# Attention with a third buffer for two copies, a second one for the inverted sums, and divisions planned later

## The chip, the cores and the metric

The kernel runs on one core of one Trainium2 chip. The number that counts is the device time of one execution, in microseconds (us). A core has a matrix engine (TensorE, "PE" in the profile, with its weight loads as "PEld"), a vector engine (VectorE, "DVE"), a scalar engine (ScalarE, "ACT"), a general one (GpSimd, "POOL") and a queue that issues transfers (SyncE, "SP"). Each works through its own list of instructions in order, and they wait for one another by semaphores.

## The reference

The input x has 2048 tokens of 576 numbers. After a layer norm two branches are computed and joined:

```
xn  = layernorm(x)
s   = attention(xn): 32 heads of 18, each token sees itself and the 255 before it
      p = softmax(q k^T / sqrt(18) in the window);  o = p v;  s = o @ wo
z   = gelu(xn @ w_in);  z1, z2 = halves of 2304 columns;  z2 = layernorm(z2)
g   = silu((z1 * (w_sp @ z2 + b_sp)) @ w_out)
out = x + s * g
```

The change lies in the attention. What matters of it: scores, their maximum, the exponential, the product P.V, and the division of P.V by the sum of the exponentials.

## The kernel before, in words

The program has stages. First q, k, v and z2 are made, until some 430 us. Then comes the attention stage, from 434 to about 884 us, in which the z1 half of `w_in` is computed as well. Then o is multiplied by `wo` (from 892 to 954 us), then come the spatial product with `w_sp` and the output product.

In the attention stage the work is cut into 16 units: 8 groups of 4 heads, times two halves of 1024 tokens (`UNITS`, `NU` = 16; the first 8 units are the first half). For each unit

- the maxima of the scores are computed ahead, 32 times a matmul (`max_item`, line 600) and a reduction on VectorE (line 604); `max_split` (613, 614) and `max_end` (623, 626) turn them into two rows that SP moves beside q (`move`, line 630);
- `scores` makes score tiles again (line 724), ScalarE takes their exponential into `pt` (line 728), GpSimd masks the diagonal and the far edge of the window (lines 736 and 739);
- `pv` multiplies with v into a PSUM tile `ops` (line 752). There is one such tile; after four blocks of tokens ScalarE copies it into one half of the unit's tile `ou` (line 767), so that a unit has two such copies. A column of ones in v gives the sums of the exponentials in the same tile;
- after the second copy `finish` plans the rest: SP takes the sums out of `ou` into `den` (814), VectorE inverts them (`invert`, 787), SP stores them (789) and reads them back spread over the partitions into `rp` (`sums`, 794), GpSimd multiplies `ou` by `rp` in four parts (`divide`, 798), and SP stores the four heads' rows to `o_d` (`store`, 803).

TensorE is filled up in between with z1: two rows of matmuls (`z1_rows`, line 671), each on half of the partitions, into one PSUM bank each (`ma` and `mb`). After 27 matmuls ScalarE copies the bank into a tile `z1o` (line 676), there are 72 such copies, and SP stores it (line 573 in the profile, where `tick` runs what is due).

The order of all this is written out when the program is built, by a planner in the same file: it keeps a clock of its own, `spend` adds TensorE's time to it, `use` keeps a planned time at which each other engine is free, and `after(ns, job)` puts a job on a list `waiting`, from which `tick` takes what is due. At each step the planner takes P.V work whose masks it believes done (`pv_now`, with the due times in `todo`), else a score or a maximum, else a matmul of z1. What comes out is a fixed order of instructions on each engine. On the chip an engine that has to wait holds all that is behind it in that order.

A tile of a pool has a number of buffers (`bufs`). When a tile is asked for again after that many times, its first writer waits until all work on the earlier tile in that buffer is done. So ScalarE's copy into `ou` of a unit waits for the stores of the unit two before it, and its copy into `z1o` for the store of the copy two before it. The work on the earlier tile must also come earlier in the program; that is what the `while parts.get(u - 2): part(u - 2)` lines are for, which put out what the planner had not yet put out.

`parts[u]` are the unit's eight late jobs, four divisions and four stores, and the times in `DIVIDE_AT` are those after the end of the unit at which they fall due, one after the other.

Of the kernel before, what the change touches and what calls it, by code (L numbers as in the profile page):

```python
# [46 lines left out]
LOAD_STEP = 700  # L47
INVERT_AT = 6500
FETCH_AT = 8500
DIVIDE_AT = (20000, 21200, 22400, 23600, 26500, 27000, 27500, 28000)  # L50
WARM = 54
SPB = 3
PTB = 5
# [6 lines left out]
def f32(ap):  # L60
    return ap.bitcast(F32)
# [3 lines left out]
def kernel(  # L65
# [170 lines left out]
    with ExitStack() as early:  # L236
# [283 lines left out]
        with ExitStack() as ph:  # L520
# [37 lines left out]
            def after(ns, fn):  # L558
                waiting.append((clock + ns, fn))
# [7 lines left out]
                return busy[engine] + drain  # L567

            def tick():
                for w in list(waiting):  # L570
                    if w[0] <= clock:
                        waiting.remove(w)
                        w[1]()
# [85 lines left out]
            def z1_rows(r):  # L659

                for f in range(FH // P):
                    z1_at[r] = f
                    if f not in z1w:
                        z1w[f] = load_z1(f)
                    wh, wl, jobs = z1w[f]
                    while jobs:
                        jobs.pop(0)[0]()
                    for b in range(2):
                        ps = fillp.tile([P, 512], F32, name=("ma", "mb")[r])
                        for n, (w, x_) in enumerate(moving_x(wh, wl, slice(b * 512, (b + 1) * 512), r)):  # L670
                            pe.matmul(ps, w, x_, start=n == 0, stop=n == STEPS - 1)  # L671
                            spend(r, MM + 3)
                            z1_done[r] += 1
                            if n == STEPS - 1:
                                zo = zw.tile([P, 512], F32, name="z1o", bufs=2)
                                act.activation(zo, ps, AF.Copy)  # L676
                                bank_free[r] = use("act", 480, 120) + 100
                                after(bank_free[r] - clock + KEEP_NS,
                                      partial(sp.dma_start, z1_tokens[f * P:(f + 1) * P, b, :, r],
                                              zo.rearrange("p (a q) -> p a q", a=2)))  # L680
                            if f + 1 < FH // P and min(z1_at) == f:
                                if b == 0 and n == 0 and f + 1 not in z1w:
                                    z1w[f + 1] = load_z1(f + 1)
                                if b == 1 and n % 4 == 2 and f + 1 in z1w and z1w[f + 1][2]:
                                    job, engine, ns = z1w[f + 1][2].pop(0)
                                    job()
                                    use(engine, ns)
                            yield
# [53 lines left out]
            def pv(u, kb, qa, qz):  # L742
                g, half = UNITS[u]
                pt = pts[u, kb]
                k0 = 0 if half == 0 else 6
                c = qa // 4
                first = max(4 * c - 2, 0)
                if kb == first:
                    o_ps[c] = ops.tile([P, 512], F32, name="ops")
                hi = min(4 * c + 3, qz)  # L750
                for j in range(4):
                    pe.matmul(o_ps[c][32 * j:32 * j + 32, (qa - 4 * c) * P:(hi - 4 * c + 1) * P],  # L752
                              vgs[u][:, kb - k0, j * VW:j * VW + 32], pt[:, j, (qa - kb) * P:(hi - kb + 1) * P],
                              start=kb == first, stop=kb == 4 * c + 3, skip_group_check=True)
                spend_both((hi - qa + 1) * 218)
                if hi == qz:
                    pts.pop((u, kb))
                else:
                    later.append([0.0, u, kb, hi + 1, qz])
                if kb == 4 * c + 3:  # L760
                    if c % 2 == 0:
                        while parts.get(u - 2):
                            part(u - 2)
                        ous[u] = (ap_.tile([P, HS], F32, name="ou", bufs=2) if u < NU - 1 else
                                  tail()[:, 0:HS])
                    ou = ous[u]
                    act.activation(ou[:, c % 2 * 512:c % 2 * 512 + 512], o_ps.pop(c), AF.Copy)
                    free_at = use("act", 500, 120)
                    for t in later:
                        t[0] = free_at  # L770
                    if c % 2 == 1:
                        finish(u, ou)
# [3 lines left out]
            def part(u):  # L776
                if parts[u]:
                    parts[u].pop(0)()

            def finish(u, ou):  # L780

                g, half = UNITS[u]
                cs = slice(half * HS, half * HS + HS)
                den = aa.tile([P, HS // 32], F32, name="den")
                rp = ap_.tile([P, HS], F32, name="rp", bufs=1) if u < NU - 1 else f32(slots[4][:, 0:HS])
                def invert():
                    dve.reciprocal(den, den)
                    t = use("dve", 270) - clock + 300
# [16 lines left out]
                if u == NU - 1:  # L805
                    def put_last():
                        dve.reciprocal(den, den)
                        sp.dma_start(r_d[u].rearrange("h (a b) -> (h a) b", b=HS // 32), den)

                    last.extend([lambda: sp.dma_start(den, ou[DH::32, :]), put_last,  # L810
                                 lambda: [sums(i) for i in range(4)], lambda: [divide(a, 2) for a in range(2)],
                                 lambda: [store(i) for i in range(4)]])
                else:
                    after(busy["act"] - clock + 1000, lambda: sp.dma_start(den, ou[DH::32, :]))
                    sooner = 10000 if u == NU - 2 else 0
                    after(max(INVERT_AT - sooner, 4500), invert)
                    parts[u] = [partial(divide, a) for a in range(4)] + [partial(store, i) for i in range(4)]
                    for ns in DIVIDE_AT:
                        after(ns - sooner + (3500 if sooner else 0), partial(part, u))

            def sp_combos(stack):

# [180 lines left out]
            with ExitStack() as heads:  # L1003
# [64 lines left out]
                while score_queue[0] or score_queue[1] or todo or filling:  # L1068
# [37 lines left out]
                        wo_splits.pop(0)()  # L1106
                    if u == NU - 1 and n % 4 == 0 and n // 4 < 5:
                        if n == 0:
                            while parts.get(u - 2):
                                part(u - 2)  # L1110
                            wors = [tail()[:, HS:HS + D],
                                    ap_.tile([P, HS], F32, name="ou", bufs=2)[:, :D]]
                        if n == 8:
                            wors.append(ap_.tile([P, 10, 89], F32, name="vg").rearrange("p a b -> p (a b)")[:, :D])
                        load_wo(n // 4)
# [572 lines left out]
```

## Time and profile before

| what | us |
|---|---|
| runs of the kernel | 1860.76, 1861.42, 1868.03; median 1861.42 |
| the profiled execution, its own time | 1859.38 |
| its span, first to last instruction | 1857.3 |
| TensorE busy in the span | 1823.3 |
| attention stage, 434 to 884 us: TensorE busy of 450.0 | 437.48 |
| mean granted clock of TensorE over the span | 0.994 |

A row of a timeline gives the start, the duration, the engine, the line of the program and the operation, `out<-in` by tile names, and in brackets how long the engine stood idle before it and on what. In a table of waits the columns are who waited for whom, the total in us, how often, and the longest. In a table of windows each engine has its busy time and its count of instructions; the last three columns are TensorE's granted clock, the share of the transfer engines that was busy, and GB/s. An engine name with a q is its queue.

### The profile page before, as it was taken

Reading aid. Unit: us, or ns where it says so; the run is one execution under the profiler, and the core shown is the slowest. Engines: PE = TensorE matmul, PEld = TensorE weight load, DVE = VectorE, ACT = ScalarE, POOL = GpSimd, SP = SyncE. Lnnn points to the kernel's source line nnn. Section 1 sums busy time; section 2 is a strip of 40 time slices with the busy share of each in tenths; the row PEclk is TensorE's granted clock in tenths of the full one; section 3 lists DMA queues with packets and bytes.
Section 4 is the critical chain, followed back from the end, with each engine's and each line's share of the span. In section 5 each row is a group of like instructions: output and inputs, shape, how many; then the busy total and the mean of one; then the engine's idle time right before and its main releaser. Section 6 shows DMA issues by size and latency. Waiting matters only on the chain.

```text
span 1857.3 us, 38172 instructions
## 1 busy us (share of the span) xinstructions
PE 1823.3 (98%) x14363; PEld 1590.3 (86%) x14363; DVE 1138.2 (61%) x2289; ACT 947.8 (51%) x1758; POOL 430.7 (23%) x507
## 2 busy tenths in 40 slices
PE   8999999999999999999999999999999999999998
PEld 8999999997777777776898878888888888899998
DVE  6321333467766677771246788667876567758876
ACT  5433322225666576667467566465554544444443
POOL 3332333334465455556100000111100000000000
PEclk9999999999999999999999999999999999999999
DMA  8885688887566666754776777789777656786554
GB/s 254 206 229 169 232 278 281 290 258 224 154 194 168 187 174 179 189 161 142 239 266 225 236 239 244 258 293 302 252 262 234 185 183 198 250 266 187 160 159 134
DMA packets 266920, 405.75 MB, mean 218 GB/s; under 512 B 52336, under 2 KB 180592, under 8 KB 266608
## 3 DMA queue, kind: packets, MB, share of 16 engines
q1 hardware_dynamic: 266736, 403.32, 70.4%
q8 instruction: 113, 1.85, 0.4%
q14 instruction: 71, 0.58, 0.1%
HBM read 285.35 MB, written 117.09 MB: 217 GB/s over the span
## 4 chain that ended last, share of the span: by engine, by line
PE 82%; DVE 7%; DMA 5%; SPq 2%; ACT 2%; issue 2%; POOL 0%; DVEq 0%; ACTq 0%; POOLq 0%
PE acc L1431 34%; PE mb L206 11%; PE c L1522 7%; PE ma L671 6%; PE mb L671 5%; PE ma L206 5%; PE ops L752 4%; PE tps L724 3%; PE sp L600 3%; PE wops L1157 2%; SPq L363 1%; DMA st_d<-qkhl 1%; DVE junk L604 1%; DVE spl L116 1%; PE ma L380 0%
## 5 line engine op out<-in xcount | busy, mean ns | idle before, releaser
L1431 PE MATMUL acc<-spl,zh 128*128 128x512 f32 x1008 | 392.6, 390 | 1.1 <-DVE spl L116 0.9
L1431 PE MATMUL acc<-sph,zh 128*128 128x512 f32 x1008 | 392.2, 389 | 0.0
L1431 PE MATMUL acc<-sph,zl 128*128 128x512 f32 x1008 | 392.1, 389 | 0.0
L604 DVE CUSTOM_DVE_ANT_0 junk<-sp,band 128x384 bf16<-128x384 f32 (+1 forms) x512 | 276.4, 540 | 114.9 <-PE sp L600 33.6
L728 ACT ACTIVATE pt<-tps 128x384 f32<-128x384 f32 (+2 forms) x576 | 231.2, 441 | 121.6 <-PE tps L724 78.0
L116 DVE TENSOR_TENSOR spl<-spr,sph 128x1024 fp32r<-128x1024 f32 x168 | 210.2, 1251 | 40.0 <-ACT sph L115 39.3
L671 PE MATMUL mb<-b,z1wh 64*128 64x512 f32 x648 | 225.2, 400 | 2.5 <-ACT z1o L676 2.1
L671 PE MATMUL ma<-b,z1wh 64*128 64x512 f32 x648 | 224.8, 399 | 0.6 <-ACT zt L948 0.4
L1431 PEld LDWEIGHTS acc<-spl,zh 128*128 128x128 f32 x1008 | 189.2, 188 | 41.7 <-DVE spl L116 2.8
L1431 PEld LDWEIGHTS acc<-sph,zh 128*128 128x128 f32 x1008 | 189.3, 188 | 39.3
L1431 PEld LDWEIGHTS acc<-sph,zl 128*128 128x128 f32 x1008 | 189.3, 188 | 39.3
L115 ACT ACTIVATE zh<-b 128x384 fp32r<-128x384 f32 x168 | 87.3, 520 | 211.1 <-PE acc L1431 206.7
L115 ACT ACTIVATE sph<-spr 128x1024 fp32r<-128x1024 f32 x168 | 176.0, 1048 | 14.5 <-DMA spr<-in_w_sp_dram 5.3
L724 PE MATMUL tps<-att 56*128 56x384 f32 (+1 forms) x576 | 177.2, 345 | 2.2 <-ACT pt L728 1.2
L116 DVE TENSOR_TENSOR zl<-b,zh 128x384 fp32r<-128x384 f32 x168 | 99.6, 593 | 124.0 <-ACT zh L115 123.9
L600 PE MATMUL sp<-att 54*128 54x384 f32 (+1 forms) x512 | 161.2, 349 | 2.0 <-DVE mx L604 1.8
L1522 PE MATMUL c<-b,o 128*128 128x288 f32 x1056 | 143.3, 295 | 0.5 <-DVE o L116 0.5
L1522 PEld LDWEIGHTS c<-b,o 128*128 128x128 f32 x1056 | 141.0, 188 | 0.8 <-DVE o L116 0.7
L949 DVE BATCH_NORM_STATS2 st<-zt 128x6 f32<-128x384 f32 x96 | 49.3, 548 | 132.1 <-ACT zt L948 132.0
L671 PE MATMUL ma<-b,z1wl 64*128 64x512 f32 x324 | 128.4, 396 | 0.0
L671 PE MATMUL mb<-b,z1wl 64*128 64x512 f32 x324 | 127.8, 394 | 0.0
L724 PEld LDWEIGHTS tps<-att 56*128 56x128 f32 x576 | 99.7, 184 | 30.5 <-issue 9.5
(219 smaller groups left out, 4189.6 us busy)
## 6 DMA issues: line engine op xcount, KB each, us to landing
spr<-sc_d SPq DMA_DIRECT2D x96, 512.0 KB
spr<-in_w_sp_dram SPq DMA_DIRECT2D x72, 512.0 KB
zr<-z_d SPq DMA_DIRECT2D x144, 192.0 KB
z_d<-zt SPq DMA_DIRECT2D x48, 384.0 KB
z_d<-z1o SPq DMA_DIRECT2D x72, 256.0 KB
z1t<-z_d SPq DMA_DIRECT2D x72, 256.0 KB
y_d<-z1t SPq DMA_DIRECT2D x72, 256.0 KB
a<-in_w_sp_dram SPq DMA_DIRECT2D x64, 256.0 KB
```

Source lines behind the costliest of these rows:

```text
L115: act.activation(hi, src, AF.Copy)
L116: dve.tensor_tensor(lo, src, f32(hi), ALU.subtract)
L206: pe.matmul(banks[h][:, :n], *both[h][i], start=i == 0, stop=i == STEPS - 1)
L600: pe.matmul(ps[:, :w], q_of(u, j)[0:54, i * P:(i + 1) * P], k_of(u, j)[0:54, k0:k0 + w], start=True, stop=True)
L604: dve.tensor_tensor_reduce(out=junk[:, :w], in0=ps[:, :w], in1=band[:, m0:m0 + w], scale=1.0, scalar=-3.0e38, op0=ALU.add, op1=ALU.max, ac ...
L671: pe.matmul(ps, w, x_, start=n == 0, stop=n == STEPS - 1)
L724: pe.matmul(ps[:, :m * P], k_of(u, j)[:, (kb - base) * P:(kb - base + 1) * P], q_of(u, j)[:, (a - lo) * P:(a - lo + m) * P], start=True, s ...
L728: act.activation(pt[:, j, d0:d0 + n * P], ps[:, (qa - a) * P:(qa - a + n) * P], AF.Exp, scale=scale)
L752: pe.matmul(o_ps[c][32 * j:32 * j + 32, (qa - 4 * c) * P:(hi - 4 * c + 1) * P], vgs[u][:, kb - k0, j * VW:j * VW + 32], pt[:, j, (qa - kb) ...
L949: dve.bn_stats(st2[:, s, pc, :], zv)
L1431: pe.matmul(acc[j], z[:, ps], w[:, cs], start=s == i == 0 and n in OPENS, stop=s == 7 and i == 2, skip_group_check=True)
L1522: pe.matmul(banks[key][:, :288], y, w, start=begin and k == n == 0, stop=close and k == 8 and n == 2, skip_group_check=True)
```

## The change

- `ou`, the copy of P.V, has three buffers and not two, `z1o`, the copy of z1, has three and not two, and `rp`, the inverted sums spread over the partitions, has two and not one. The lines that put out late jobs before a buffer is taken again go by the unit three back for `ou`, and a new line puts out the divisions of the unit two back before `rp` is taken.
- The four divisions of a unit fall due 24.0 to 27.6 us behind its end and not 20.0 to 23.6, its four stores 33 to 36 us behind and not 26.5 to 28.0. For the unit before the last (`sooner`) the divisions keep their times, 13.5 to 17.1, and the stores come at 22.5 to 25.5 and not at 20.0 to 21.5.
- At the start of the last unit the parts put out are those of unit 12 and not of unit 13; the second tile there for a piece of `wo` is one of the three `ou` buffers.
- `tick` takes what is due in the order of the due times and not in the order in which it was put on the list.

```diff
-DIVIDE_AT = (20000, 21200, 22400, 23600, 26500, 27000, 27500, 28000)
+DIVIDE_AT = (24000, 25200, 26400, 27600, 33000, 34000, 35000, 36000)
...
             def tick():
-                for w in list(waiting):
+                for w in sorted(waiting, key=lambda w: w[0]):
...
-                                zo = zw.tile([P, 512], F32, name="z1o", bufs=2)
+                                zo = zw.tile([P, 512], F32, name="z1o", bufs=3)
...
-                        while parts.get(u - 2):
-                            part(u - 2)
-                        ous[u] = (ap_.tile([P, HS], F32, name="ou", bufs=2) if u < NU - 1 else
+                        while parts.get(u - 3):
+                            part(u - 3)
+                        ous[u] = (ap_.tile([P, HS], F32, name="ou", bufs=3) if u < NU - 1 else
...
+                while len(parts.get(u - 2, ())) > 4:
+                    part(u - 2)
                 den = aa.tile([P, HS // 32], F32, name="den")
-                rp = ap_.tile([P, HS], F32, name="rp", bufs=1) if u < NU - 1 else f32(slots[4][:, 0:HS])
+                rp = ap_.tile([P, HS], F32, name="rp", bufs=2) if u < NU - 1 else f32(slots[4][:, 0:HS])
...
                     for ns in DIVIDE_AT:
-                        after(ns - sooner + (3500 if sooner else 0), partial(part, u))
+                        after(ns - (10500 if sooner else 0), partial(part, u))
...
-                            while parts.get(u - 2):
-                                part(u - 2)
+                            while parts.get(u - 3):
+                                part(u - 3)
                             wors = [tail()[:, HS:HS + D],
-                                    ap_.tile([P, HS], F32, name="ou", bufs=2)[:, :D]]
+                                    ap_.tile([P, HS], F32, name="ou", bufs=3)[:, :D]]
```

## The prediction

> **What bounds the kernel now.** I read the page's busy times first, then windows over the attention stage, where the whole change lies, then TensorE's waits in that stage, and then the timeline around each of them.
>
> ```profile
> PE 1823.3 (98%) x14363; PEld 1590.3 (86%) x14363; DVE 1138.2 (61%) x2289; ACT 947.8 (51%) x1758; POOL 430.7 (23%) x507
> ...
> 434.00:884.00 450.00, 437.48 (x4316) 333.79 (x4316) 287.28 (x1022) 298.08 (x734) 238.56 (x350) 1.00 0.63 174
> ...
> PE sp L623 <- DVE ms L614: 2.9, 5, 0.9
> PE mb L671 <- ACT z1o L676: 2.1, 4, 1.5
> PE ops L752 <- ACT ou L767: 2.0, 2, 1.1
> PE ops L752 <- issue: 1.7, 2, 0.9
> PE tps L724 <- ACT pt L728: 1.2, 3, 0.8
> PE ops L752 <- POOL ou L798: 0.8, 1, 0.8
> PE tps L724 <- DMA att<-mhl: 0.7, 1, 0.7
> ```
>
> TensorE is the bound, and its order is fixed when the program is built. In the attention stage it stood idle for 450.0 - 437.5 = 12.5 us, and no change that leaves TensorE's work as it is can win more there than that and what a lower clock costs. The change adds no instruction and removes none: it moves 120 of them and takes waits for buffers away. So the question is which of the waits above are waits for a buffer. The names on the right don't say it, since ScalarE and GpSimd are themselves held up by something. Two of the waits are.
>
> The first is the longest of the two behind `ACT ou`:
>
> ```profile
> 583.89 0.32 SPq L803 DMA_DIRECT2D o_d<-ou  x1
> ...
> 589.73 0.60 ACT L767 ACTIVATE ou<-ops 128x512 f32<-128x512 f32 x1 [1.29 <-DMA r_d<-den]
> ...
> 590.38 0.86 PE L752 MATMUL ops<-pt,vg 128*32 128x128 f32 x16 [1.11 <-ACT ou L767]
> ```
>
> ScalarE's copy at 589.73 is the first of unit 5, into the buffer that unit 3 used. It waited 1.29 us for a transfer. The profile names the store of the inverted sums, but a copy into `ou` needs nothing of those; what it needs is that the last store out of that buffer has landed, the one issued at 583.89. So that store took 5.8 us to land or a little less, and TensorE lost 1.11 us.
>
> The second is the longest behind `ACT z1o`:
>
> ```profile
> 628.19 0.60 ACT L676 ACTIVATE z1o<-mb 128x512 f32<-128x512 f32 x1 [4.33 <-PE mb L671]
> 628.83 0.60 ACT L676 ACTIVATE z1o<-ma 128x512 f32<-128x512 f32 x1
> ...
> 633.32 7.21 DMA z_d<-z1o
> ...
> 640.63 0.60 ACT L676 ACTIVATE z1o<-mb 128x512 f32<-128x512 f32 x1 [1.60 <-DMA z_d<-z1o]
> ...
> 641.28 0.49 PE L671 MATMUL mb<-b,z1wh 64*128 64x512 f32 x1 [1.54 <-ACT z1o L676]
> ...
> 642.00:643.00 1.00, 1.00 (x8) 0.88 (x7) 0.45 (x3) 1.00 (x3) 0.00 (x1) 0.59 0.59 181
> 643.00:644.00 1.00, 1.00 (x8) 0.85 (x8) 0.54 (x2) 1.00 (x3) 1.00 (x2) 0.50 0.70 194
> 644.00:645.00 1.00, 1.00 (x8) 1.00 (x6) 0.57 (x2) 0.60 (x3) 1.00 (x2) 0.50 0.70 111
> 645.00:646.00 1.00, 1.00 (x10) 0.95 (x7) 0.36 (x1) 0.50 (x2) 0.19 (x1) 0.70 1.33 189
> ```
>
> The copies at 628.19 and 628.83 took both buffers. The store of the first was issued at 633.32, 4.5 us after that copy ended, and took 7.21 us. The third copy had to wait, and TensorE, whose bank it was to empty, stood for 1.54 us. Then the granted clock (third number from the right) was below one in four windows: they lost 0.41 + 0.50 + 0.50 + 0.30 = 1.71 us of full clock. I count both to this wait: 3.25 us.
>
> The rest of the waits are of other kinds. These rows look like GpSimd's and like nobody's:
>
> ```profile
> 666.03 0.43 PE L752 MATMUL ops<-pt,vg 128*32 128x128 f32 x8 [0.76 <-POOL ou L798]
> ...
> 721.22 0.60 ACT L767 ACTIVATE ou<-ops 128x512 f32<-128x512 f32 x1
> ...
> 721.93 0.86 PE L752 MATMUL ops<-pt,vg 128*32 128x128 f32 x16 [0.89 <-issue]
> ```
>
> At 721.93 TensorE began the next unit's P.V 0.11 us after ScalarE had emptied the only `ops` tile (721.22 + 0.60 = 721.82). The wait at 666.03 is of the same kind: same line, the first P.V of a unit of the second half. It belongs to the one `ops` tile, which the change leaves, whatever name stands behind it. So I don't count it as won, though its label names a division.
>
> **The change part by part.**
>
> *Third buffer of `ou`.* It frees a copy from the stores of the unit two back. 30 copies run from 460.2 to 857.0 us (row of the tile below), 13.7 us apart on the mean, 27.4 us a unit. A copy into a third-back buffer comes about 2 x 27.4 + 13.7 = 68 us behind that unit's end; the last store is now planned 36 us behind it, and with 6 us of landing is over by 42. With two buffers and the new times it would have been 42 against 41, a stall in every unit: the later stores need the third buffer. Won: 1.11 us. Added: no instruction.
>
> *Third buffer of `z1o`.* The 72 copies come in pairs, one pair in 450 / 36 = 12.5 us. The copy at 640.63 would have used the buffer of the copy before that at 628.19, a pair further back, so it doesn't wait for a store issued at 633.32. Won: 1.54 us, and 1.71 with the clock. The Trainium skill, in "TensorE: Matmul & The Clock Gate", section "Why this matters for your kernels", asks only that there be no idle gap of TensorE beyond about 3 us; by that rule a gap of 1.54 us would not have brought the clock down, the slow stretch would stay, and the sum below would be 2.65 and not 4.36. The trace shows half clock right behind a gap half as long, so here I side with the rows.
>
> *Divisions and stores later.*
>
> ```profile
> L798 POOL TENSOR_TENSOR ou<-ou,rp x60: 722/738/1247, 500.7 to 877.9; 128x256 f32<-128x256 f32 x60
> L803 SPq DMA_DIRECT2D o_d<-ou x60: 264/314/1267, 508.2 to 880.2; - x60
> L767 ACT ACTIVATE ou<-ops x30: 592/598/633, 460.2 to 857.0; 128x512 f32<-128x512 f32 x30
> ...
> L798 POOL TENSOR_TENSOR ou<-ou,rp 128x256 f32<-128x256 f32 x60 | 43.6, 747 | 15.9 <-DMA rp<-r_d 9.9 <-DMA z_d<-z1o 4.4 <-DMA att<-st_d 1.5
> ...
> POOL ou L798 <- DMA rp<-r_d: 9.9, 5, 3.0
> ...
> POOL ou L798 <- DMA z_d<-z1o: 4.4, 1, 4.4
> ...
> SPq L803 <- POOL ou L798: 20.1, 6, 8.1
> ...
> 580.00:590.00 10.00, 9.26 (x96) 6.57 (x92) 7.23 (x28) 5.69 (x13) 4.59 (x8) 1.00 0.80 209
> ...
> 600.00:610.00 10.00, 10.00 (x97) 7.64 (x93) 6.56 (x27) 7.98 (x19) 6.39 (x10) 1.00 0.78 211
> ```
>
> 56 divisions of 14 units move by 4 us and 56 stores by 6.5 to 8 us; unit 14 keeps its divisions, and its stores come 2.5 to 4 us later. GpSimd stood 15.9 us before divisions, mostly for `rp`, with the masks behind it in its queue. The longest single ones were 3.0 and 4.4 us, so with the divisions 4 us later nearly all of the 15.9 goes. For TensorE I count nothing: none of its waits above names a mask. SP stood 20.1 us before stores with K, Q and the moved maxima behind it; with 8.4 to 9 us planned between a division and its store, where there were 4.4 to 6.5, that goes too. Again TensorE had only 0.7 us on a move. Neither is in the sum; both are gains that may show.
>
> What it may cost: four divisions are 4 x 0.747 = 3.0 us of GpSimd, now planned from 24 us on, that is, around the next unit's end at 27.4, among that unit's last masks. The windows show room: GpSimd is busy 4.6 and 6.4 of 10 us. The planner knows each division's price and holds P.V back for it, so TensorE's order changes. That is the unknown. Its bound: single waits of this stage are 0.7 to 1.5 us and all sum to 12.5; a new order may lose or win about a third of that, 4 us either way. I take zero, since the rows favour neither sign. On SP a store costs 0.314 us to issue, four of them 1.3 us. They leave the place behind the `den` load and the K and Q loads and come 6 to 9 us behind the next unit's end, beside the store of the inverted sums and ahead of the moves of the maxima. No wait of TensorE there exceeds 0.7 us. If that cover goes, each unit's moves come up to 1.3 us late.
>
> *Second buffer of `rp`, the new and changed loops, the sorted list.* `rp` is loaded some 15 us behind a unit's end (6.5 + 8.5, `INVERT_AT` and `FETCH_AT`), so the next unit's load comes 42 us behind this one's, after the divisions in either case; the buffer only lets the order be written. The loops find nothing left to put out. Sorting swaps jobs that fall due in the same step. Zero.
>
> *Start of the last unit.* Before, all of unit 13 was put out at once:
>
> ```profile
> 849.07 0.39 SPq L573 DMA_DIRECT2D z_d<-z1o  x1
> 857.60 1.35 SPq L803 DMA_DIRECT2D o_d<-ou  x4
> 859.04 0.37 SPq L996 DMA_DIRECT2D att<-in_wo_dram  x1
> ```
>
> SP stood until 857.60, its longest wait (8.1), with a piece of `wo` behind it. Now that piece goes out some 5 us earlier and unit 13's stores some 10 later. Neither is needed before the product with `wo` at 892. Zero.
>
> *The sum.* 1.11 + 1.54 + 1.71 = 4.36 us. The profiled execution took 1859.38, so 1855.0; the median of the runs lies 2.04 above that execution, which gives 1857.06. I say 1857.0.
>
> **The rivals.** A difference under 0.5% (9.3 us) is about what a measurement of this kernel can't tell from no change.
>
> *New waits take the place of the old.* The new order brings five more waits like that at 721.93, 0.89 us each: 4.45 us, 1861.5. For it: that kind of wait comes by itself in an order that a planner wrote without it. Against: nothing in the change makes them likelier.
>
> *The slow clock stays,* because it answered to the thin stretch of work around 640 us and not to the gap: 1859.38 - 2.65 + 2.04 = 1858.8. The Trainium skill's rule on the clock gate, named above, points the same way.
>
> *Slower: a division in front of the last masks.* GpSimd's divisions now straddle the unit's end. If in each of 14 units one of them (0.747) holds the mask for which the last P.V waits, TensorE loses 10.5 us: 1861.4 - 4.4 + 10.5 = 1867.5. It outweighs the gain from six units on. For it: the place. Against: the planner's price for a division is 725 ns, near the 747 measured, and GpSimd has 3.6 us in ten free or more.
>
> *Larger gain.* GpSimd's and SP's freed waits reach TensorE: then the waits of P.V (2.0 + 1.7 + 0.8), of `mb` (2.1), of the moves (0.7) and the clock go, 9.0 us: 1852.4. Against: the `ops` tile explains most of the P.V waits.
>
> *The gain is lost on the way to 916 us.*
>
> ```profile
> 886.18 6.60 DMA att<-o_d
> ...
> 896.90 4.57 DMA att<-r_d
> ...
> 901.69 3.62 POOL att L798 x2
> ...
> 916.66 37.04 PE wops L1157 x276
> ```
>
> The chain from the last unit's P.V to the product with its rows goes through transfers, but it starts from that P.V, which moves with TensorE. If it didn't, the time would be 1861.4, as with the first rival.
>
> **How the numbers follow.** Forecast 0.53; new waits or a lost gain 0.22 (1861.5, give or take 3); slow clock stays 0.08; slower 0.08; larger gain 0.09. The forecast's own range, with half the bound on the new order, is 1854 to 1860.5. From 1851.5 to 1864.5 the range holds all but most of the slower case and the far ends. Faster by over 0.5% means below 1852.1: half of the larger gain, 0.05. Slower by over 0.5% means above 1870.7: the slower case with more than one division a unit, 0.04. Within: 0.91.
>
> **What the changed profile should show.** Among ScalarE's waits no copy `ou` or `z1o` behind a transfer; `PE mb <- ACT z1o` near 0.6; no window below full clock between 434 and 884 us; TensorE idle there near 9.9 us. The wait of GpSimd before divisions falls from 15.9 to under 4, that of SP's stores from 20.1 to under 8. The first division starts near 504.7, the first store near 514. `PE ops` waits of 0.8 to 1.1 at the first P.V of some units stay. I am wrong if the stage's idle time doesn't fall, if `PE ops` waits for masks (L736, L739) appear at the units' ends, or if the slow windows stay without a gap before them.

## The result, and the profile after

The changed kernel takes 1868.01 us (median of 22 runs, 1864.04 to 1871.82), the kernel before 1861.47 in the same comparison (22 runs). The ratio is 1.0034, 95% interval 1.0025 to 1.0043: slower by some 6.3 us, less than the 0.5% that the prediction took as its bound, but outside its range of 1851.5 to 1864.5. The interval is under 0.1% to either side, so differences far below 0.5% can be told from none here. The profiled execution took 1869.05 us with a span of 1867.3.

The page's busy time of TensorE:

```profile
PE 1829.7 (98%) x14363; PEld 1593.3 (85%) x14363; DVE 1137.5 (61%) x2289; ACT 946.8 (51%) x1758; POOL 431.3 (23%) x507
```

The same 14363 matmuls took 6.4 us more of TensorE's time than before. Windows of the changed kernel, the attention stage and two stretches in it (the last three columns: clock, share of the transfer engines, GB/s):

```profile
434.00:884.00 450.00, 436.36 (x4268) 337.37 (x4268) 289.17 (x1029) 294.25 (x725) 237.22 (x348) 0.98 0.66 174
...
622.00:630.00 8.00, 8.00 (x63) 4.29 (x60) 4.38 (x15) 3.95 (x9) 1.22 (x2) 0.57 0.32 104
680.00:685.00 5.00, 5.00 (x24) 3.95 (x22) 3.40 (x13) 2.63 (x6) 0.13 (x1) 0.66 0.44 148
```

TensorE's idle time in the stage did not fall (13.6 us, 12.5 before), and the clock is below one in more places than before: 8 x 0.43 = 3.4 us of full clock are lost from 622 on and 5 x 0.34 = 1.7 us from 680 on. TensorE's waits from 434 to 900 us:

```profile
PE sp L600 <- DVE mx L604: 7.0, 2, 3.8
PE sp L623 <- DVE ms L614: 3.5, 4, 1.8
PE tps L724 <- DMA att<-mhl: 2.0, 1, 2.0
PE tps L724 <- ACT pt L728: 0.3, 1, 0.3
PE ma L671 <- ACT z1o L676: 0.2, 1, 0.2
```

The waits for a buffer of `ou` and `z1o` are gone but for 0.2 us, and with them all waits for the `ops` tile. In their place stands a wait that had 0.3 us in all before: TensorE, with scores for the maxima to make, has no free tile because VectorE doesn't read them, twice for more than 3 us. What VectorE waited for, over the whole run, first before and then after:

```profile
DVE den L787 <- DMA den<-ou: 31.7, 6, 27.4
```

```profile
DVE den L789 <- DMA den<-ou: 36.7, 6, 20.9
```

The longest in each is that of unit 14, where VectorE has nothing else to do. Without it VectorE stood 4.3 us before inversions, and now 15.8. The timeline after, the rows of VectorE and of TensorE in units 3, 5 and 7:

```profile
566.39 0.35 DVE L789 RECIPROCAL den<-den 128x32 f32<-128x32 f32 x1 [2.59 <-DMA den<-ou]
...
569.58 0.30 PE L623 MATMUL sp<-ident,ms 128*64 128x128 f32 x1 [1.80 <-DVE ms L614]
...
620.52 0.35 DVE L789 RECIPROCAL den<-den 128x32 f32<-128x32 f32 x1 [5.83 <-DMA den<-ou]
...
621.35 0.44 PE L600 MATMUL sp<-att 54*128 54x384 f32 x1 [3.83 <-DVE mx L604]
...
678.94 0.35 DVE L789 RECIPROCAL den<-den 128x32 f32<-128x32 f32 x1 [4.96 <-DMA den<-ou]
...
679.77 0.44 PE L600 MATMUL sp<-att 54*128 54x384 f32 x1 [3.15 <-DVE mx L604]
```

Each row of TensorE comes behind an inversion: VectorE stands before the inversion until `den` is there, the next maxima stand behind it in VectorE's order, and TensorE runs out of tiles: in unit 5 VectorE stopped at 620.52 - 5.83 = 614.69 and TensorE 2.8 us later, in unit 7 2.6 us later. Behind the gaps of 3.83 and 3.15 us comes the slow clock of the two windows above.

To compare kernels with one another I use one stretch: from the end of the first copy into `ou` to the end of the product with `wo`. It holds the same 4615 matmuls in every kernel, and leaves out the time before it, in which the kernels do the same and single executions differ by some us. Windows over that stretch, before and after:

```profile
460.81:953.70 492.89, 480.85 (x4615) 379.07 (x4612) 288.88 (x979) 315.10 (x746) 233.11 (x339) 1.00 0.64 182
```

```profile
464.08:962.75 498.67, 486.22 (x4615) 386.39 (x4612) 287.01 (x978) 313.98 (x746) 232.19 (x339) 0.99 0.65 179
```

It became 5.8 us longer. The rest of the 10.0 us between the two spans is 3.3 us ahead of the stretch and some 1 behind it.

### The profile page after: what moved, and what is told of

It is laid out like the page before. It is cut to its first block, busy times and chain, and to the rows that moved or that the text cites. A ratio compares the mean times of both kernels' runs of the same rounds, so it can differ in the third digit from the quotient of the medians.

```text
span 1867.3 us, 38158 instructions
## 1 busy us (share of the span) xinstructions
PE 1829.7 (98%) x14363; PEld 1593.3 (85%) x14363; DVE 1137.5 (61%) x2289; ACT 946.8 (51%) x1758; POOL 431.3 (23%) x507
## 4 chain that ended last, share of the span: by engine, by line
PE 84%; DVE 7%; DMA 5%; SPq 2%; ACT 2%; issue 1%; POOL 0%; DVEq 0%; ACTq 0%
PE acc L1433 34%; PE mb L206 9%; PE c L1524 7%; PE ma L206 6%; PE ma L671 6%; PE mb L671 6%; PE ops L752 4%; PE tps L724 3%; PE wops L1159 3%; PE sp L600 3%; SPq L363 1%; DMA den<-ou 1%; DMA st_d<-qkhl 1%; PE ma L380 1%; DVE junk L604 1%
```

## The experiments

Every kernel was timed side by side with the kernel before, and the ratio is of those times. They come from five sessions, in which the kernel before had medians of 1860.33 to 1862.22, so medians of different sessions can differ by 1 to 2 us for that reason alone; the row "before" is that of the first. "Stretch" is the one just described, from the profile; idle is its length less TensorE's busy time; "slow clock" is the sum of one less the clock over its windows of 1 us; "VectorE" is its wait before the inversions of units 0 to 13. The last three columns come from one execution each, and can be off by some us where the ratio isn't.

| kernel | ratio, 95% interval | median us | stretch us | against before | idle / slow clock / VectorE us |
|---|---|---|---|---|---|
| before | | 1861.47 | 492.89 | | 12.0 / 1.7 / 4.3 |
| after | 1.0034 [1.0025, 1.0043] | 1868.01 | 498.67 | +5.8 | 12.5 / 5.1 / 15.8 |
| rings | 0.9974 [0.9961, 0.9986] | 1857.19 | 488.10 | -4.8 | 9.2 / 0.0 / 8.5 |
| z1o_alone | 1.0008 [0.9998, 1.0017] | 1862.02 | 490.66 | -2.2 | 11.6 / 0.0 / 4.0 |
| ou_rp_alone | 0.9996 [0.9985, 1.0007] | 1859.68 | 491.26 | -1.6 | 10.7 / 1.7 / 6.0 |
| times_new_order_old | 0.9985 [0.9973, 0.9998] | 1858.93 | 491.95 | -0.9 | 12.5 / 0.0 / 8.7 |
| times_old_order_new | 1.0033 [1.0020, 1.0046] | 1869.06 | 499.27 | +6.4 | 13.1 / 6.8 / 17.8 |
| invert_late_order_kept | 0.9967 [0.9955, 0.9979] | 1856.49 | 488.89 | -4.0 | 6.2 / 1.7 / 1.3 |
| rings_invert_early | 1.0112 [1.0091, 1.0132] | 1880.42 | 511.05 | +18.2 | 22.4 / 8.5 / 23.2 |
| order_old_invert_late | 0.9994 [0.9982, 1.0006] | 1859.36 | 493.51 | +0.6 | 12.5 / 1.7 / 0.8 |
| z1w_behind_den | 0.9991 [0.9979, 1.0003] | 1859.06 | 495.12 | +2.2 | 8.9 / 5.1 / 11.1 |
| both_cures | 0.9978 [0.9967, 0.9988] | 1858.25 | 492.64 | -0.3 | 8.2 / 1.7 / 0.0 |
| den_own_queue | 1.051 [1.0492, 1.0528] | 1954.51 | 584.65 | +91.8 | 76.7 / not summed / not compared |

The mean clock of every single run is on record too, and bears out what the two traces show of it: 0.9925 over the 22 runs of the changed kernel, and 0.9955 to 0.9957 over the 17 to 23 runs of the kernel before in the four later sessions. The difference of 0.003 over 1867 us is some 6 us of full clock. With the old times and the new order it is 0.9923, with the inversion early 0.9912, with the inversion late in the new order 0.9957 again.

My theory when I had seen the two traces: the buffers gained what the prediction says, and the new order, which the planner made when the divisions' price fell later, lost more by VectorE's wait for `den`. Rivals: the positions of the divisions and stores on GpSimd's and SP's queues cost it, or the new order of TensorE is worse by itself.

### The buffers alone

The changed kernel with the old times, the old list and the old place for unit 13's parts. The order of every engine is then that of before.

```diff
-DIVIDE_AT = (24000, 25200, 26400, 27600, 33000, 34000, 35000, 36000)
+DIVIDE_AT = (20000, 21200, 22400, 23600, 26500, 27000, 27500, 28000)
-                for w in sorted(waiting, key=lambda w: w[0]):
+                for w in list(waiting):
-                        after(ns - (10500 if sooner else 0), partial(part, u))
+                        after(ns - sooner + (3500 if sooner else 0), partial(part, u))
-                            while parts.get(u - 3):        # start of the last unit
-                                part(u - 3)
+                            while parts.get(u - 2):
+                                part(u - 2)
```

> The buffers alone: three for ou and z1o, two for rp, with the divisions, the stores and the order of every engine as before. Theory A (the prediction's step: two waits for buffers cost 1.11 + 1.54 us and a slow clock 1.71): about 1857, ratio to before 0.9977, and no copy of ScalarE behind a transfer. Rival (the waits only show up elsewhere): 1861.5, ratio 1.000.

Windows over the stretch, and TensorE's waits from 434 to 900 us:

```profile
460.27:948.37 488.10, 478.87 (x4615) 377.84 (x4612) 288.26 (x979) 314.96 (x747) 233.08 (x339) 1.00 0.66 184
```

```profile
PE mb L671 <- ACT z1o L676: 1.0, 4, 0.3
PE ops L752 <- ACT ou L767: 0.9, 1, 0.9
```

The time is 1857.19, where the kernel before had 1860.94 in the same session; by the ratio the gain is 4.8 us (2.6 to 7.3). The stretch is 4.8 us shorter than before: 2.8 of idle time, 1.7 of clock, 0.3 of other busy time. No wait of 1.1 or 1.5 us for `ou` or `z1o` is left, and no window of the stretch is below full clock. From here to the changed kernel are 10.8 us in the medians and 10.6 in the stretch: 3.2 more idle, 5.1 more of slow clock, and 2.2 of busy time beside the clock that I can't assign.

### Order and times, each without the other

The divisions and stores stand where one of the kernels has them, and the planner books the divisions' price on GpSimd where the other has them, so that the order of TensorE, VectorE and ScalarE is that of the other.

```diff
+CHARGE_AT = (20000, 21200, 22400, 23600, 26500, 27000, 27500, 28000)
...
                     pool.tensor_tensor(ou[:, hs], ou[:, hs], rp[:, hs], ALU.mult)
-                    use("pool", 2900 / n)
...
+                    for ns in CHARGE_AT:
+                        after(ns - sooner + (3500 if sooner else 0), partial(charge, u))
                     for ns in DIVIDE_AT:
                         after(ns - (10500 if sooner else 0), partial(part, u))
```

Here `charge` books `use("pool", 2900 / 4)`; this is the first kernel, and in the second the two lists and their offsets change places.

> Buffers and the later divisions and stores as in the changed kernel, but the planner charges GpSimd's time for a division at the old due times, so that TensorE, VectorE and ScalarE have exactly the order of before; only GpSimd's and SP's lists change. Theory B (the new order of the work costs the time): about 1857 to 1859, ratio 0.998, and VectorE's waits for the sums (den) stay near the 4.3 us of before in the first 14 units. Theory C (the divisions and stores cost it by the places they have moved to, on SP and in the transfers): 1866 to 1868, ratio 1.003, waits for den near 15 us.

> The converse: TensorE, VectorE and ScalarE in exactly the order of the changed kernel, the buffers too, but divisions and stores at the old times behind a unit. Theory B: 1866 to 1868, ratio 1.003, with VectorE waiting some 15 us for den in units 3, 5 and 7 again. Theory C: 1857 to 1860, ratio 0.998, waits for den near 4 us.

With the new times and the old order the kernel is still faster than before (0.9985, against 0.9974 of the buffers alone); with the old times and the new order nearly the whole loss is there (1.0033, the changed kernel 1.0034). TensorE's waits in the second:

```profile
PE sp L601 <- DVE mx L605: 7.9, 4, 4.4
PE sp L624 <- DVE ms L615: 3.8, 5, 1.3
```

These are the waits of the changed kernel, without its later divisions. So the places of the divisions and the stores cost 1.7 us or nothing (the intervals of the buffers alone and of the new times overlap), and the order some 10 us. Both of these kernels take the due jobs in the sorted order, so the sorting is not what costs the time.

### The inversion later in the new order

In the changed kernel VectorE's inversion, with the store and the loads of `rp` that follow it, is put 3.5 us (the loads 3 us) later; TensorE's, ScalarE's and GpSimd's orders are kept.

```diff
-FETCH_AT = 8500
+FETCH_AT = 8000
...
                     dve.reciprocal(den, den)
-                    t = use("dve", 270) - clock + 300
+                    t = max(busy["dve"] - clock, 200) + 570
...
-                    after(max(INVERT_AT - sooner, 4500), invert)
+                    after(max(INVERT_AT - sooner, 4500), lambda: use("dve", 270))
+                    after(max(INVERT_AT - sooner, 4500) + (0 if sooner else 3500), invert)
```

> The changed kernel with the inversion of the sums 3.5 us later on VectorE (10 us behind a unit and not 6.5) and the fetch of rp 3 us later, the order of TensorE, ScalarE and GpSimd as in the changed kernel. If VectorE standing before the inversion, with the maxima behind it, is what costs the time (units 3, 5 and 7: 2.6, 5.8 and 5.0 us of VectorE, 1.8, 3.8 and 3.2 us of TensorE and a slow clock behind each), these fall to 0, 2.3 and 1.5 us and the time to 1858 to 1861, ratio 0.999. If those waits only cover something else: 1866 to 1868, ratio 1.003.

VectorE's wait before inversions and TensorE's waits:

```profile
DVE den L789 <- DMA den<-ou: 22.0, 2, 20.7
```

```profile
PE sp L623 <- DVE ms L614: 2.5, 4, 0.9
PE ops L752 <- POOL pt L739: 1.9, 2, 1.3
```

The time is 1856.49: with TensorE's order unchanged, 11.5 us are back, and the waits of TensorE at line 600 (7.0 us) are gone. SP's store and loads moved along in this edit; the next run moves VectorE's instruction alone. The new order is not slow in itself; it is slow with the inversion where it stood. This kernel beats the one before by 0.33% (0.21 to 0.45); it and the buffers alone can't be told apart.

### The converse: the inversion earlier in the old order

The kernel with the buffers alone, in which the inversion of units 0 to 13 stands 2.5 us earlier in VectorE's order and nothing else moves.

```diff
                 def invert():
-                    dve.reciprocal(den, den)
+                    if u == NU - 2:
+                        dve.reciprocal(den, den)
...
+                    if not sooner:
+                        after(max(4000, busy["act"] - clock + 1300), lambda: dve.reciprocal(den, den))
                     after(max(INVERT_AT - sooner, 4500), invert)
```

> The kernel with the buffers alone (order of before on every engine, 1857.2 us), in which one thing is moved: VectorE's inversion stands 2.5 us earlier in VectorE's order in units 0 to 13; SP's, TensorE's, ScalarE's and GpSimd's orders are kept. Theory (what costs the time is VectorE standing before the inversion with maxima behind it): the data lands when it landed, so VectorE waits some 2.5 us longer in each of 14 units, 8.5 + 35 = 43 us in all instead of 8.5; TensorE loses what lies beyond about 2 us of it in a unit, 1 to 2 us in most units, and the clock drops behind the longer ones: 1870 to 1895. Rival (the new order of TensorE is worse in itself, and VectorE's wait only goes along with it): TensorE's order is that of the fast kernel, so the time stays within 1855 to 1861.

VectorE's wait before these inversions and TensorE's longest wait:

```profile
DVE den L820 <- DMA den<-ou: 23.2, 10, 4.8
```

```profile
PE sp L600 <- DVE mx L604: 13.5, 9, 4.1
```

The fast order became slow: 1880.42, 23.2 us above the buffers alone (by the ratios some 26), from one instruction moved a little in each unit. VectorE's wait grew by 14.7 us, less than the 35 I expected, since it does not reach the inversion 2.5 us sooner in all units; yet the stretch grew by 23.0, of which 13.2 are idle time, 8.5 slow clock and 1.2 other busy time. A us of VectorE's wait here cost more than a us: its 14.7 us came with 13.2 us of TensorE's idle time and 8.5 us of slow clock.

### The inversion later in the old order

The kernel with new times and old order, with the same edit of the inversion as above.

> The kernel with divisions and stores at their new times and the order of TensorE, ScalarE and VectorE of before (1858.9 us), in which the inversion and the store and the loads of rp behind it stand 3 to 3.5 us later in units 0 to 13. If an inversion that VectorE never waits for is worth something in the old order too: VectorE's wait before inversions (8.7 us in its first 14 units) falls below 3, TensorE's waits for maxima (2.6 + 2.1 us) to under 3 in all, and the time is 1854 to 1857.5. Rival (only waits beyond about 2 us reach TensorE, and the old order has one such): no difference that can be measured, 1857.5 to 1860.5.

Nothing was gained (0.9994 against 0.9985; the rival's range). VectorE's wait went from 8.7 to 0.8 us, but TensorE had hardly waited for it there: its waits for maxima went from 4.7 us to 2.3, and 1.8 us of waits for masks came in. The edit mends only an order in which VectorE's waits reach TensorE.

### Why `den` is late: ScalarE's queue

What holds `den` up? SP's rows of the changed kernel around unit 5, whose second copy ended at 608.35:

```profile
610.04 0.36 SPq L640 DMA_DIRECT2D z1raw<-in_w_z_dram  x1
610.93 0.29 SPq L550 DMA_DIRECT2D att<-st_d  x1
611.45 0.38 SPq L573 DMA_DIRECT2D z_d<-z1o  x1
612.19 0.30 SPq L550 DMA_DIRECT2D att<-st_d  x1
612.96 0.62 SPq L816 DMA_DIRECT2D den<-ou  x1
```

SP issues one transfer every 0.5 to 1 us, and `den` 4.6 us behind the copy. Ahead of it stand K and Q loads and the next z1 weights (576 KB). I first moved `den`'s load to another queue:

```diff
-                    after(busy["act"] - clock + 1000, lambda: sp.dma_start(den, ou[DH::32, :]))
+                    after(busy["act"] - clock + 1000, lambda: act.dma_start(den, ou[DH::32, :]))
```

> The changed kernel with one edit: the load of the sums into den is issued on ScalarE's queue instead of SP's, at the same place of the program; the order of TensorE, VectorE and GpSimd is that of the changed kernel, and SP's and ScalarE's differ by these loads alone. Theory (den is late because its load stands in SP's queue behind the K and Q loads and the z1 weights): in units 3, 5 and 7 the inversion starts 6 to 7.5 us behind the copy instead of 9.3, 12.2 and 10.9, VectorE's wait before inversions falls from 15.8 us (the harmless one of unit 14 left out) to under 4, TensorE's waits for maxima (7.0 and 3.5 us) to under 4 in all, and the time is 1855.5 to 1860. Rival (the transfer is slow wherever it is issued, because the transfer engines are loaded): den still lands 5 to 7 us behind its issue in those units, and the time stays within 3 us of 1868.

It took 1954.51, 87 us more than the changed kernel, which neither side expected. The waits of ScalarE from 434 to 900 us, and of TensorE:

```profile
ACT pt L728 <- DMA att<-st_d: 66.9, 10, 8.6
```

```profile
PE tps L724 <- ACT pt L728: 73.2, 13, 8.3
```

The timeline in unit 5, SP's queue and ScalarE's:

```profile
637.78 0.36 SPq L640 DMA_DIRECT2D z1raw<-in_w_z_dram  x1
638.31 0.29 SPq L550 DMA_DIRECT2D att<-st_d  x1
639.22 0.38 SPq L573 DMA_DIRECT2D z_d<-z1o  x1
639.65 2.20 SPq L550 DMA_DIRECT2D att<-st_d  x4
642.10 0.38 SPq L699 DMA_DIRECT2D vg<-v_d  x1
...
644.30 0.55 ACTq L816 DMA_DIRECT2D den<-ou  x1
644.95 0.87 ACT L728 ACTIVATE pt<-tps 128x384 f32<-128x384 f32 x2 [8.04 <-DMA z1raw<-in_w_z_dram]
```

ScalarE stood 8 us with the exponentials behind it, for a load that SP had issued. From the z1 weights' load at 637.78 to `den`'s at 644.30 are eight transfers. In the event records of the trace the run's 1615 transfers use eight semaphores in turn, 201 or 202 each, whichever queue they are on, and here a transfer starts when the eighth before it has landed; `den`'s waited on that of the z1 weights, which came at 644.20, 6.4 us after their issue. So here `den` was held by what was in flight ahead of it and not by SP. As a test of what a late `den` costs VectorE the run says nothing, since ScalarE's waits cover all else.

### Why `den` is late: the load of the z1 weights

In the changed kernel SP has the load of the next z1 weights four to nine places ahead of `den` in units 3, 5 and 7, the three with the long waits. Here those three loads are issued right behind `den`; no other engine's order changes.

```diff
-                sp.dma_start(raw, w_z1[f])
+                if f in (6, 8, 10):
+                    after(5500, lambda: sp.dma_start(raw, w_z1[f]))
+                else:
+                    sp.dma_start(raw, w_z1[f])
```

> The changed kernel with three transfers moved: in units 3, 5 and 7, where SP issues the load of the next z1 weights four to nine places ahead of the load of den, it is issued right behind it. Nothing else on any engine moves; no work is left out. Theory (in the new order these three loads fall just ahead of den, SP holds den's load for them, the inversion comes late and VectorE's maxima behind it): in these units the inversion starts 6.5 to 8.5 us behind the copy instead of 9.3, 12.2 and 10.9, VectorE's waits before inversions fall from 15.8 us (unit 14 left out) to 3 to 6, TensorE's waits for maxima from 7.0 us to under 3, and the time is 1856 to 1861. Rival (it is the K and Q loads ahead of den, or the load of the transfer engines, that makes den late): the waits and 1868 stay, within 3 us.

The inversions of units 5 and 7, and TensorE's waits:

```profile
619.32 0.35 DVE L792 RECIPROCAL den<-den 128x32 f32<-128x32 f32 x1 [2.62 <-DMA den<-ou]
...
674.55 0.35 DVE L792 RECIPROCAL den<-den 128x32 f32<-128x32 f32 x1 [4.35 <-DMA den<-ou]
```

```profile
PE sp L600 <- DVE mx L604: 3.2, 2, 2.5
PE tps L727 <- ACT pt L731: 3.1, 3, 2.0
PE sp L623 <- DVE ms L614: 1.8, 3, 0.9
```

The time is 1859.06, 9 us below the changed kernel (8 by the ratios), by three transfers moved. The execution traced is one of the longest of the twelve, 1863.41 us with a clock of 0.992 where their mean is 0.995, so that its stretch is only 3.6 us shorter than that of the changed kernel; the rows tell where `den` comes from, and less of what the edit is worth. In unit 3 `den` was issued 2.0 us behind the copy and not 4.2, and VectorE's wait fell from 2.59 to 0.74. In unit 5 it was issued as late as before (4.8), but the inversion came 4.2 us behind the issue and not 7.6: with the weights ahead of it the transfer itself took longer. In unit 7 little changed (4.96 to 4.35): there ten K and Q loads in a row and four more stand ahead, and `den` was issued 5.6 us behind the copy in both. So the weights' load is the cause in unit 3 and of over half of the wait in unit 5, and VectorE's wait fell only to 11.1 us, not to the 3 to 6 expected. Unit 7 I put down to the K and Q loads, which was not tried. The edit has a price too: the weights land later, and TensorE waits 3.1 us for ScalarE, where it was 0.3.

### Both edits together

The changed kernel with the three loads behind `den` and the later inversion.

> The changed kernel with the inversion 3.5 us later (1856.5 us by itself) and the three loads of z1 weights behind den as well (1859.1 by itself). Theory (both edits act on one cost, VectorE's wait before the inversion, and the later inversion had already taken it away): VectorE's waits before inversions stay below 2 us, unit 14 left out, and the time is that of the later inversion alone, 1855 to 1858. Rival (the two edits save different things, 11.5 and 9 us): 1850 or less.

VectorE's waits before inversions, all of them:

```profile
DVE den L792 <- DMA den<-ou: 20.7, 1, 20.7
```

Only the wait of unit 14 is left, and the time is 1858.25, not below the later inversion alone: the median lies 0.25 above the range that I gave, and far from the rival's. The two edits save the same thing. That the second brings its price along is likely (TensorE waits 4.2 us for ScalarE here, and 1.1 with the later inversion alone), but the intervals of the two ratios overlap.

### The two buffers apart

```diff
-                                zo = zw.tile([P, 512], F32, name="z1o", bufs=2)
+                                zo = zw.tile([P, 512], F32, name="z1o", bufs=3)
```

> The kernel before with the third buffer of z1o and nothing else; the order of every engine is that of before. By the prediction's terms 1.54 us of wait and 1.71 us of slow clock go and the 1.11 us wait at the copy into ou stays: 1861.4 - 3.25 = 1858.2, that is 1.1 above the kernel with the buffers alone (1857.2); ScalarE's copy into ou of unit 5 still waits some 1.3 us for a transfer, and no copy into z1o does. Rival (the slow clock around 643 us belongs to the thin stretch of work, not to the gap): windows below full clock stay there, and the time is 1859 to 1860.

And the buffers alone with `z1o` back at two:

```diff
-                                zo = zw.tile([P, 512], F32, name="z1o", bufs=3)
+                                zo = zw.tile([P, 512], F32, name="z1o", bufs=2)
```

> The kernel before with the third buffer of ou and the second of rp; z1o keeps two buffers, and the order of every engine is that of before. By the prediction's terms only the 1.11 us wait at the copy into ou goes: 1860.3, the waits at 641.28 and the slow windows behind it stay, TensorE's time from the first copy into ou to the end of the product with wo falls by 1 to 2 us against before's 492.9. Rival (the buffers of z1o gained nothing and those of ou and rp all of it): 1856.5 to 1858, with the wait for z1o still there.

With `z1o` alone, ScalarE's waits, TensorE's waits, and the window of the place where the clock was slow:

```profile
ACT ou L767 <- DMA att<-st_d: 1.7, 1, 1.7
```

```profile
PE ops L752 <- ACT ou L767: 2.3, 2, 1.5
```

```profile
640.00:650.00 10.00, 10.00 (x95) 7.75 (x92) 7.71 (x27) 7.46 (x18) 4.75 (x8) 1.00 0.75 214
```

The slow windows are gone with the gap in this trace and the wait for `ou` is still there, as the theory has it; the stretch is 2.2 us shorter. With `ou` and `rp` it is 1.6 shorter, `PE ops <- ACT ou` fell to one wait of 0.9, and a slow stretch of 1.7 us came at 916, in the product with `wo`. The two add up to 3.8, near the 4.8 of both.

The times do not show it: z1o alone is no faster (0.9998 to 1.0017, where 0.9983 was expected), `ou` and `rp` 0.9985 to 1.0007, and both together 0.9974. By these ratios the parts add up to a loss of under 1 us and the whole gains 4.8. One reason is on record: the traced execution of z1o alone has the highest clock of its eleven runs, 0.998, where the others have 0.992 to 0.996. Their mean is 0.9950 and that of the kernel before in the same session 0.9957, so over all runs z1o alone lost no less clock. And in the same trace a gap of nearly the old length has full clock behind it:

```profile
593.45 0.64 PE L752 MATMUL ops<-pt,vg 128*32 128x128 f32 x12 [1.47 <-ACT ou L767]
```

Where in the other runs the clock was lost can't be told from a mean.

## Why the prediction was wrong

**The waits for buffers: right as a sum, open in its parts.** The sum was 1.11 + 1.54 + 1.71 = 4.36 us. The buffers alone gained 4.8 us by the ratio (2.6 to 7.3), 3.8 between the medians of their own session, and 4.8 in the stretch; both waits are gone in the changed kernel too. But the interval reaches down to the 2.65 us of the two waits without the clock, and z1o alone, which should have brought 3.25 of the 4.36, brought nothing that the times show. That the slow clock belonged to the gap of 1.54 us, and not to the thin work of the second rival, is what the trace of z1o alone agrees with; its other runs don't bear it out, and a gap of 1.47 us in it cost no clock. So the term of 1.71 us is not shown, and that the sum came out may in part be luck.

**The new order of TensorE: the step that failed.** "The planner knows each division's price and holds P.V back for it, so TensorE's order changes. That is the unknown [...] I take zero, since the rows favour neither sign", with a bound of 4 us either way. It cost 10.6 to 10.8 us (the stretch, the medians), over two and a half times the bound. The bound was made from the sizes of the waits that the old order had. But a new order brings waits of a kind that the old one had in small: `den`'s wait by VectorE stood in the old trace with 4.3 us in units 0 to 13 (2.04 us in unit 5), and the prediction didn't look at it, since next to none of it reached TensorE:

```profile
613.26 0.35 DVE L787 RECIPROCAL den<-den 128x32 f32<-128x32 f32 x1 [2.04 <-DMA den<-ou]
```

What hid it was, as far as the rows of the changed kernel tell, the work that TensorE still had when VectorE stopped, 2.6 to 2.8 us. In the new order z1's weights are asked for at other moments, in units 3 and 5 eight and four places ahead of `den`, and the waits of 5 to 6 us in units 5 and 7 go beyond that cover. The bound also left the clock out: 5.1 of the 10.6 us are slow clock behind two gaps.

**The slower rival: near in size by chance, wrong in place.** It gave 1867.5, beside the measured 1868.01, by GpSimd's divisions in front of masks. No wait of TensorE for a mask is among those after, and with old times and new order the loss is there without the later divisions. The engine that held TensorE was VectorE.

**Divisions and stores later.** The groups of `ou`'s instructions after (count, shortest, median and longest in ns, first and last start):

```profile
L800 POOL TENSOR_TENSOR ou<-ou,rp x60: 723/737/1245, 505.9 to 884.4; 128x256 f32<-128x256 f32 x60
L805 SPq DMA_DIRECT2D o_d<-ou x60: 264/295/1566, 513.7 to 888.3; - x60
```

The waits of GpSimd and of SP's queue after:

```profile
POOL ou L800 <- DMA rp<-r_d: 2.4, 1, 2.4
```

```profile
SPq L805 <- DMA att<-st_d: 10.4, 19, 1.4
SPq L805 <- DMA vg<-v_d: 7.1, 4, 2.4
SPq L805 <- POOL ou L800: 1.8, 1, 1.8
```

GpSimd's wait before divisions fell from 15.9 to 2.4 us (predicted: under 4), SP's for a division from 20.1 to 1.8 (under 8), the first store came at 513.7 (514), the first division at 505.9 (504.7). That neither gain would reach TensorE was right: new times in the old order gained nothing on the buffers alone. But SP's stores now wait 17.5 us for earlier transfers, which I hadn't counted; they had 6.2 of that kind from z1 weights and K and Q loads before.

**The other signs.** The waits of TensorE for the `ops` tile, which should have stayed, are all gone: they were no property of the tile but of the old order, at the places where it put the next P.V right behind the copy. Slow windows appeared behind gaps, as before, and not without one. That the stage's idle time doesn't fall was named as a sign of being wrong, and it rose, from 12.5 to 13.6 us. The change stayed within 0.5%, which had the chance 0.91, but by a gain of some 5 us and a loss of some 11, and not as reckoned.

**The profiled execution.** It also lost 2.0 us at the first move of maxima (`att<-mhl`), ahead of every division, with 1.7 us of slow clock behind it. The kernel with `ou` and `rp` alone, in the old order, has the same wait with 2.5 us, so it is not the new order's.

## What to carry to other kernels

When a planner writes the order, a change of a price or a due time is a change of every engine's order; bound it by the waits that the old order just barely hides (the small waits of engines that are not the bound, for transfers with little slack), not by those that already reach the bounding engine. An instruction that waits for a transfer should stand in its engine's order well behind the time at which that transfer lands on a bad occasion, above all where the engine has work behind it that feeds the bound. And look at the clock behind each gap of TensorE: here half clock came behind some and not behind others, and made up about half of the loss.

## What the runs showed that I had not expected

- The slow clock comes in pieces of a size. Added up over its windows, each slow stretch cost 1.7 us of full clock or 3.4; the clock records of the traces have half clock for 3.41 or 6.83 us each time there (and for 10.24 in the run with `den` on ScalarE's queue). It was 1.7 behind gaps of 1.54 us (before, 642 us) and of 3.15 us (after, 680 us), and 3.4 behind one of 3.83 us (after, 622 us), but also behind one of 1.99 us (the z1 weights behind `den`, 568 us). Behind the gaps of 1.80 us at 569.58 (after), of 1.47 us at 593.45 (z1o alone) and of 2.06 us at 748.73 (the inversion early) there was none. So between 1.5 and 2.1 us the length alone doesn't decide, and what does the runs don't tell. The Trainium skill, "TensorE: Matmul & The Clock Gate", section "HAM oscillation — how this bites in real kernels", gives the rule as no idle gap above some 3.4 us. The stretches here fit that length (1.7 us lost at half clock is 3.4 us of time), but half clock also came right behind gaps of half of it, so by these traces the rule is too lenient.
- A transfer issued from ScalarE waited for transfers that SP had issued, 66.9 us in ten waits: in this program the limit of eight in flight goes with its semaphores and not with the queue.
- A load of 16 KB (`den`, 128 x 32 numbers) took 7.6 us from its issue to the inversion with a load of 576 KB issued 2.9 us ahead of it, and 4.2 us with that load behind it.
